# An attention, MoE and gated-MLP kernel: the first 768 tokens of its last layer by plain products in place of seven block products

## The chip, the cores and the metric

The kernel runs on one core of a Trainium2 chip. The metric is the device time of one execution in microseconds (us). The engines are TensorE (PE, its weight loads PEld), VectorE (DVE), ScalarE (ACT), GpSimd (POOL) and SyncE (SP), whose queue issues nearly all DMAs; each runs its own instructions in order.

## The reference

Windowed causal attention (4 x 8 heads, 576 tokens, head width 64) gives x, 2304 tokens x 512. Then come two feed-forward layers:

```python
# MoE1: 8 experts, each with the 288 tokens that the routing gives it
h = np.maximum(x[mask] @ w1[e], 0.0)      # 512 -> 1024
out[mask] = h @ w2[e]                     # 1024 -> 512
# MoE2: all 2304 tokens; its weights w_in, w_out arrive as 64-bit floats
h = x @ w_in                              # 512 -> 2048
g = h * (1.0 / (1.0 + np.exp(-h)))        # silu
return (g @ w_out).astype(np.float32)     # 2048 -> 512
```

## The kernel before

**Arithmetic.** Every float32 operand of a matmul is split into a high and a low part (`hi` by a ScalarE copy, `lo` by a VectorE subtraction), and a product takes three matmuls (`three`, L613 to L615; `unit`, L832).

**MoE1** (`moe1`) runs over 8 experts x 8 chunks of the hidden layer. A chunk (512 KB: a piece of w1 and one of w2) is loaded into a `raw` tile, split (`fetch`, L587 to L590, in a ring of 5 tiles), multiplied with the expert's 288 tokens (`first`, 12 matmuls, L762), put through relu (L765, L766), and two chunks later multiplied by its w2 piece (`second`, 12 matmuls of 288 columns). At each expert's end four accumulators are copied out (L783 on VectorE, L785 on ScalarE, two each) and stored to `yd` in DRAM.

**64-bit weights.** MoE2's 16 chunks are 64-bit. `fetch64` makes float32 of half a chunk: a 512 KB load (L600), then four VectorE operations (L604, L605, L606, L608) and one ScalarE Square (L607). Twelve chunks are converted during MoE1, one in every five steps, and kept in SBUF (`keep`, 12 tiles); four are converted during MoE2's group 0 (`late`) and go to `wd` in DRAM (L678), from where `chunk` reloads them (L667). The load, a `raw` tile, shares four `raw` slots with the chunks of MoE1, the block weights' temporary `s`, reloaded chunks and the output tiles.

**MoE2** (`moe2`) takes the tokens in three groups of 768. x @ w_in is made by seven block products instead of eight: `split_y` makes seven operands of a group's tokens (B11, B21, T1 to T4, B22; subtractions at L654, parts at L657 and L658), `split_w` seven of a pair of chunks (f and f + 8; sums on GpSimd L696 to L699, parts L692, L693). In group 0 `split_w` computes them and stores them to `wx` (L702, L703); groups 1 and 2 load them from there (L705, L706). A step (g, f) has seven products of 6 matmuls with 384 columns, in the order 0, 1, 3, 2, 4, 5, 6, in two PSUM tiles `pa` and `pb`; between them VectorE adds up the blocks (L890 to L907), so a product can't start before the sum over the product that last used its PSUM tile. Two silus of 768 columns follow (`silu`: sigmoid L848, product L849, copy L851, subtraction L852). Each step leaves 12 units (3 matmuls of 512 columns each, accumulating g @ w_out) in a list `todo`; `fill` runs them between the products of the next step:

```python
product(0, pa); ...; product(1, pb); fill(2)
product(3, pa); ...; fill(3)
product(2, pb); product(4, pa); ...; fill(4)
product(5, pa); product(6, pb); ...; fill(3)
```

Group 0's first step has no units pending; its products 0 and 1 are issued in MoE1, before the last `second`. A group's last units copy out the accumulators and scatter them to the output (L839 to L843).

**Order.** A planner places the instructions on each engine by its own estimate of times, in program order where it sees no better; instructions under `keep_in_program_order` stay in order among themselves. Each engine, and SP's queue, then runs that list strictly in order.

Of the kernel before, what the change touches and what calls it, by code (L numbers as in the profile page):

```python
# [20 lines left out]
P = 128  # L21
# [3 lines left out]
E = 8  # L25
# [596 lines left out]
HF = FC2 // 2  # L622
SOON = 6
BUSY_G = (14, 3, 3, 6)


class Halves:
# [19 lines left out]

    def split_y(self, n, sub=None):

        nc, b = self.tc.nc, self.b  # L650
        name = self.ORDER[n][1]
        for t, x, y, at in (("T1", "B12", "B11", "B11"), ("T2", "B22", "T1", "T1"), ("T3", "B22", "B12", "B12"), ("T4", "B21", "T2", "T2")):
            if name == t:
                (sub or nc.gpsimd).tensor_tensor(b[at], b[x], b[y], ALU.subtract)  # L654
                b[t] = b[at]
        hi, lo = (self.pool.tile([P, 2, HT], F32R, name=name + x) for x in "hl")
        nc.scalar.copy(hi, b[name])  # L657
        nc.vector.tensor_tensor(lo, b[name], hi, ALU.subtract)  # L658
        self.y[name] = hi, lo

    def chunk(self, c, n):

        q = slice(512 * n, 512 * n + 512)
        if c % HF < SOON:
            return self.f32[c][:, q]
        r = self.wts.raw.tile([P, 512], F32, name="raw")
        self.tc.nc.sync.dma_start(r, self.wd[c % HF - SOON + (HF - SOON) * (c // HF)][:, q])  # L667
        return r

    def convert(self, c):  # L670

        kept = c % HF < SOON
        r = self.f32[c] = self.wts.keep.tile([P, 1024], F32, name="w32") if kept else self.wts.raw.tile([P, 1024], F32, name="raw")
        self.wts.fetch64(c, r, (0,))
        yield
        self.wts.fetch64(c, r, (1,))
        if not kept:
            self.tc.nc.sync.dma_start(self.wd[c % HF - SOON + (HF - SOON) * (c // HF)], r)  # L678
# [39 lines left out]
def moe(tc, wts, xtab, idx96, k, hv, by128, idx128, out):  # L718
    nc = tc.nc
    with tc.tile_pool(name="ph", bufs=1, space=PSUM) as ph, tc.tile_pool(name="py", bufs=1, space=PSUM) as py, \  # L720
            tc.tile_pool(name="px", bufs=2, space=PSUM) as px:
        pp = [ph.tile([P, 512], F32, name=f"p{i}") for i in range(2)]
        w = moe1(tc, wts, xtab, idx96, k, hv, by128, pp, py, px)
        moe2(tc, wts, hv, w, idx128, out, pp, py, px)


def moe1(tc, wts, xtab, idx96, k, hv, by128, pp, py, px):
# [3 lines left out]
    with tc.tile_pool(name="m1", bufs=2) as m1:  # L731
# [39 lines left out]
        def second(e, f, h):  # L771
# [44 lines left out]
    return w0  # L816


def moe2(tc, wts, hv, w, idx128, out, pp, py, px):
    nc = tc.nc  # L820
    with tc.tile_pool(name="m2", bufs=1) as m2:
        obs = {}

        outs = dram_disjoint_views(out, NT)

        def unit(accs, g, f, blk, gg, z, d):

            (gh, gl), (hi, lo) = gg, z
            q = slice(d % 3 * P, d % 3 * P + P)
            start, stop = f == 0 and blk in (0, 1), f == HF - 1 and blk in (2, 3)  # L830
            for i, (x, y) in enumerate(((gh, hi), (gl, hi), (gh, lo))):
                tc.keep_in_program_order(nc.tensor.matmul(accs[d], x[:, q], y, start=start and i == 0, stop=stop and i == 2))  # L832
            if stop:
                if (g, d // 2) not in obs:
                    obs[g, d // 2] = wts.raw.tile([P, 2, 512], F32, name="raw")
                ob = obs[g, d // 2][:, d % 2]
                cut = 256 if f + 1 == HF and g + 1 == NG and d == 5 else 512 * (1 - d % 2)
                if cut:
# [6 lines left out]
        def silu(x):  # L845
# [20 lines left out]

        steps = [(g, f) for g in range(NG) for f in range(HF)]
        late = (x for i in range(2 * (HF - SOON)) for x in hv.convert(SOON + i // 2 + HF * (i % 2)))
        for i, (g, f) in enumerate(steps):
            if f == 0:  # L870
                accs = [py.tile([P, 512], F32, name=f"y{d}") if d < 4 else px.tile([P, 512], F32, name="pt") for d in range(6)]
            pa, pb = (p[:, 0:HT] for p in pp)

            def product(n, p):
                hv.product(n, p, w)
                if f == HF - 1 and g + 1 < NG:

                    for j in {2: (2, 3), 3: ()}.get(n, (n,)):
                        hv.split_y(j)

            if i:
                product(0, pa)
            u = hv.pool.tile([P, HT], F32, name="u")
            nc.scalar.copy(u, pa)
            if i:
                product(1, pb)
            fill(2)
# [22 lines left out]
            h21, h12 = silu(xb)  # L910
            order = [(0, h11, za, 0), (1, h22, zb, 3), (2, h21, zb, 0), (3, h12, za, 3)]
            if i + 1 < len(steps):
                w = hv.split_w(*steps[i + 1])
                todo += [(accs, g, f, b, h, z, d0 + d) for b, h, z, d0 in order for d in range(3)]
            else:

                for b, d in ((0, 0), (0, 1), (1, 3), (2, 0), (3, 3), (0, 2), (2, 1), (1, 4), (3, 4), (2, 2), (1, 5), (3, 5)):
                    _, h, z, d0 = order[b]
                    unit(accs, g, f, b, h, z, d)
            if g == 0:  # L920
                for _ in range((2, 1, 1, 2, 1, 1, 0, 0)[f]):
                    next(late)
            if f == 2 and g + 1 < NG:
                hv.load_y(g + 1)


@with_exitstack
def fused(ctx, tc, qT, kT, vA, vT, wg, w32, w64, rel, cst, out):
# [30 lines left out]
    c3.close()  # L959
    wts.keep = ctx.enter_context(tc.tile_pool(name="keep", bufs=2 * SOON))  # L960
# [3 lines left out]
    hv.wd = dram.tile([2 * (HF - SOON), P, 1024], F32, name="wd")  # L964

# [49 lines left out]
```

## Time and profile before

| | |
|---|---|
| median of 3 runs | 832.88 us (831.89 to 833.85) |
| profiled execution | 832.89 us |
| its span, first to last instruction | 831.1 us |
| mean granted TensorE clock | 0.969 of 2.4 GHz |
| MoE1 | 200.8 to 430.1 us of the span |
| MoE2, group 0 / 1 / 2 | from 430.1 / 560.2 / 688.2 us, last matmul near 824 us |

A stage here begins with its first matmul, and group 0's with the end of MoE1's last one. "Busy" TensorE includes overlapped matmuls, so the pace of a stage is read from the distance of its matmuls. "Idle before" is idle time of the engine ahead of an instruction, with what ended it.

### The profile page before, as it was taken

Reading aid. Unit: us, or ns where it says so; the run is one execution under the profiler, and the core shown is the slowest. Engines: PE = TensorE matmul, PEld = TensorE weight load, DVE = VectorE, ACT = ScalarE, POOL = GpSimd, SP = SyncE. Lnnn points to the kernel's source line nnn. Section 1 sums busy time; section 2 is a strip of 40 time slices with the busy share of each in tenths; the row PEclk is TensorE's granted clock in tenths of the full one; section 3 lists DMA queues with packets and bytes.
Section 4 is the critical chain, followed back from the end, with each engine's and each line's share of the span. In section 5 each row is a group of like instructions: output and inputs, shape, how many; then the busy total and the mean of one; then the engine's idle time right before and its main releaser. Section 6 shows DMA issues by size and latency. Waiting matters only on the chain.

```text
span 831.1 us, 13442 instructions
## 1 busy us (share of the span) xinstructions
PE 785.6 (95%) x4885; PEld 711.1 (86%) x4885; DVE 609.0 (73%) x1372; ACT 379.2 (46%) x659; POOL 219.8 (26%) x229
## 2 busy tenths in 40 slices
PE   7999999997999999999988999999999999999996
PEld 5899998746999999999977888888889888889885
DVE  7999899463677789887798897798555488556553
ACT  4967777202555554554544543454233245223222
POOL 3879799404011012000052111134000023100002
PEclk8999999597999999999998999999999999999999
DMA  9999773302686787778756355546534223723202
GB/s 233 292 249 239 204 216 110 123 2 71 196 271 221 234 305 237 238 268 295 249 183 251 140 205 172 193 173 215 207 100 167 89 88 131 262 90 137 92 0 77
DMA packets 48822, 150.14 MB, mean 181 GB/s; under 512 B 5808, under 2 KB 10416, under 8 KB 45680
## 3 DMA queue, kind: packets, MB, share of 16 engines
q1 hardware_dynamic: 45776, 139.79, 52.3%
q0 software_dynamic: 2976, 9.44, 3.3%
q8 instruction: 41, 0.67, 0.3%
q14 instruction: 29, 0.24, 0.1%
HBM read 118.28 MB, written 30.93 MB: 180 GB/s over the span
## 4 chain that ended last, share of the span: by engine, by line
PE 39%; DVE 17%; DMA 13%; issue 3%; ACT 3%; SPq 0%; POOLq 0%; POOL 0%; ACTq 0%; DVEq 0%
PE y L832 11%; DMA raw<-w 11%; PE pt L832 6%; PE p L613 5%; PE p L615 5%; PE p L614 5%; PE p L762 4%; DVE w L590 2%; DVE gl L852 2%; DVE w L693 2%; ACT w L589 2%; DVE bits L605 1%; DVE bits L606 1%; DVE sg L849 1%; PE y L614 1%
## 5 line engine op out<-in xcount | busy, mean ns | idle before, releaser
L832 PE MATMUL y<-z,gh 128*128 128x512 f32 x384 | 135.8, 395 | 0.0
L590 DVE TENSOR_TENSOR w<-raw,w 128x1024 fp32r<-128x1024 f32 x60 | 73.9, 1231 | 33.1 <-ACT w L589 32.6
L762 PE MATMUL p<-xh,w 128*128 128x288 f32 x512 | 82.3, 300 | 8.0 <-DVE hl L766 7.7
L589 ACT CAST w<-raw 128x1024 fp32r<-128x1024 f32 x60 | 63.0, 1049 | 55.7 <-DMA raw<-w 42.0
L832 PEld LDWEIGHTS y<-z,gh 128*128 128x128 f32 x384 | 72.6, 189 | 13.4 <-ACT gh L851 0.2
L762 PEld LDWEIGHTS p<-xh,w 128*128 128x128 f32 x512 | 72.0, 190 | 10.3 <-DVE hl L766 9.5
L832 PE MATMUL y<-z,gl 128*128 128x512 f32 x192 | 76.6, 399 | 3.5 <-DVE gl L852 3.5
L848 ACT ACTIVATE sg<-xa 128x768 f32<-128x768 f32 x24 | 20.3, 846 | 124.0 <-DVE xa L901 123.9
L614 PE MATMUL y<-hl,w 128*128 128x288 f32 x256 | 74.6, 298 | 0.6 <-DVE hl L766 0.6
L615 PE MATMUL y<-hh,w 128*128 128x288 f32 x256 | 73.9, 295 | 0.0
L832 PE MATMUL pt<-z,gh 128*128 128x512 f32 x192 | 71.2, 392 | 0.0
L613 PE MATMUL y<-hh,w 128*128 128x288 f32 x256 | 67.8, 300 | 1.5 <-ACT yo L785 1.1
L742 POOL DMA_INDIRECT xg<-xtab,idx x24 | 26.0, 1084 | 131.9 <-PE pt L746 123.0
L237 ACT ACTIVATE pe<-sc,mx 128x128 f32<-128x128 f32 x144 | 47.8, 395 | 20.7 <-DVE mx L235 20.4
L843 POOL DMA_INDIRECT out<-raw,idx x18 | 19.8, 1099 | 135.1 <-ACT raw L839 130.9
L852 DVE TENSOR_TENSOR gl<-sg,gh 128x768 fp32r<-128x768 f32 x48 | 52.4, 1092 | 2.2 <-ACT gh L851 2.2
L260 PE MATMUL po<-va,pc 128*128 128x73 f32 x256 | 53.0, 291 | 0.0
L260 PE MATMUL po<-va,pp 128*128 128x73 f32 x256 | 52.4, 289 | 0.3 <-DVE va L206 0.2
L614 PEld LDWEIGHTS y<-hl,w 128*128 128x128 f32 x256 | 48.5, 189 | 0.8 <-DVE hl L766 0.8
L654 POOL TENSOR_TENSOR yr<-yr 128x768 f32<-128x768 f32 x8 | 17.3, 2156 | 120.5 <-issue 92.6
L615 PEld LDWEIGHTS y<-hh,w 128*128 128x128 f32 x256 | 48.5, 189 | 0.0
L227 PE MATMUL pss<-khh,qs 128*128 128x256 f32 (+1 forms) x144 | 43.4, 322 | 4.0 <-DVE qs L141 3.6
(266 smaller groups left out, 2148.1 us busy)
## 6 DMA issues: line engine op xcount, KB each, us to landing
raw<-w SPq DMA_DIRECT2D x96, 512.0 KB, 4.8
w<-wx SPq DMA_DIRECT2D x16, 1024.0 KB, 4.9
w<-wx SPq DMA_DIRECT2D x16, 768.0 KB, 6.8
kr<-kT SPq DMA_DIRECT2D x35, 256.0 KB, 5.4
wx<-w SPq DMA_DIRECT2D x8, 1024.0 KB, 4.9
wx<-w SPq DMA_DIRECT2D x8, 768.0 KB, 5.1
va<-vA SPq DMA_DIRECT2D x18, 292.0 KB, 5.2
qr<-qT SPq DMA_DIRECT2D x18, 256.0 KB, 5.8
```

Of the source, the lines that this page charges most:

```text
L227: nc.tensor.matmul(pss[:, j, :nb, :], qs[:, h, :], kk[:, first:first + (nb - 1) * st + 1:st, h, :], start=(i == 0), stop=(i == 1))
L237: nc.scalar.activation(pe[:, i, :], sc[:, i, :], AF.Exp, bias=mx[:, i:i + 1], scale=-1.0)
L260: nc.tensor.matmul(po[:, j, :], w[:, j, :], va[:, s, 4 * g + j, :], start=(i == 0), stop=(i == nb - 1))
L589: nc.scalar.copy(hi, r)
L590: nc.vector.tensor_tensor(lo, r, hi, ALU.subtract)
L613: keep(tc.nc.tensor.matmul(out, whi, xhi, start=start, stop=False))
L614: keep(tc.nc.tensor.matmul(out, whi, xlo, start=False, stop=False))
L615: keep(tc.nc.tensor.matmul(out, wlo, xhi, start=False, stop=stop))
L742: nc.gpsimd.indirect_dma_start(xg, None, xtab, bass.IndirectOffsetOnAxis(ap=idx96[:, e * PER + j:e * PER + j + 1], axis=0))
L762: nc.tensor.matmul(p, w[:, dc * P:dc * P + P], x[:, dc, :], start=(i + dc == 0), stop=(i == 2 and dc == DC - 1))
L832: tc.keep_in_program_order(nc.tensor.matmul(accs[d], x[:, q], y, start=start and i == 0, stop=stop and i == 2))
L852: nc.vector.tensor_tensor(gl, sg, gh, ALU.subtract)
```

## The change

Group 0 of MoE2 no longer uses block products. It runs over the 16 chunks j; for each half t of the 768 tokens `plain` makes 12 matmuls of 384 columns, then come 3 units, and a silu of 384 columns (`silu1`), whose 3 units run after the next half's product. The chunk's split parts come from `fetch`, which now goes on past MoE1's 64 chunks. The seven operands of the tokens and `split_w`'s sums are made for group 1 first; group 0 needs four parts of its tokens without subtractions (`part_y`). Eight chunks (0 to 7) are converted in MoE1, one in seven steps, with load tiles of their own (two in the pool `m1`), and kept; the other eight are converted during group 0, 16 halves spread over j = 0 to 12, and all go to `wd`. `raw` has five slots. In MoE1 all four output copies are ScalarE's. Each output tile of MoE2 has a `raw` slot of its own instead of half of one. Operands B11 and B21 of a next group get a second buffer and are made two steps before its start.

```diff
     def fetch(self, upto):
-        while self.next < min(upto, E * FC1):
+        while self.next < min(upto, NW):
             i = self.next
-            r = self.raw.tile([P, 1024], F32, name="raw")
-            nc.sync.dma_start(r, self.w32[i])
+            if i < E * FC1:
+                r = self.raw.tile([P, 1024], F32, name="raw")
+                nc.sync.dma_start(r, self.w32[i])
+            else:
+                r = self.f32[i - E * FC1]
             hi, lo = self.parts(self.ring)
...
-    def fetch64(self, i, dst, halves=(0, 1)):
+    def fetch64(self, i, dst, raw, halves=(0, 1)):
...
-            r = self.raw.tile([P, 512, 2], I32, name="raw")
+            r = raw.tile([P, 512, 2], I32, name="raw")
...
-SOON = 6
+SOON = 8
...
+    def part_y(self, name, room=None):
+        nc = self.tc.nc
+        hi, lo = (self.pool.tile([P, 2, HT], F32R, name=(room or name) + x, bufs=2 if name in ("B11", "B21") else 1) for x in "hl")
+        nc.scalar.copy(hi, self.b[name])
+        nc.vector.tensor_tensor(lo, self.b[name], hi, ALU.subtract)
+        self.new[name] = hi, lo
...
     def chunk(self, c, n):
-        if c % HF < SOON:
-            return self.f32[c][:, q]
+        if c < SOON:
+            return self.wts.f32[c][:, q]
...
+    def plain(self, j, out, w, t):
+        hi, lo = w
+        for i in range(2):
+            yh, yl = self.y[f"B{i + 1}{t + 1}"]
+            for dc in range(2):
+                q = slice((2 * i + dc) * P, (2 * i + dc) * P + P)
+                three(self.tc, out, hi[:, q], lo[:, q], yh[:, dc], yl[:, dc], i + dc == 0, i + dc == 2, True)
...
     def split_w(self, g, f):
-        if g == 0:
+        if g == 1:
...
 def moe1(tc, wts, xtab, idx96, k, hv, by128, pp, py, px):
...
                 for d in range(DC):
-                    if d % 2:
-                        nc.vector.tensor_copy(yo[:, d], ys[e][d])
-                    else:
-                        nc.scalar.copy(yo[:, d], ys[e][d])
+                    nc.scalar.copy(yo[:, d], ys[e][d])
...
-                if n % 5 == 4 and n // 10 < SOON:
-                    for _ in hv.convert(n // 10 + HF * (n // 5 % 2)):
+                if n % 7 == 4 and n // 7 < SOON:
+                    for _ in hv.convert(n // 7, m1):
...
-                if n > 44 and n % 2 and n // 2 < 22 + 7:
-                    hv.split_y(n // 2 - 22, nc.vector)
-                if n == E * FC1 - 2:
-                    w0 = hv.split_w(0, 0)
+                if n in (46, 50, 54, 58):
+                    x = ("B11", "B21", "B12", "B22")[(n - 46) // 4]
+                    hv.part_y(x, "T4" if x == "B12" else None)
...
-        hv.product(0, pp[0][:, 0:HT], w0)
-        hv.product(1, pp[1][:, 0:HT], w0)
+        hv.plain(0, pp[0][:, 0:HT], wts.ready[E * FC1], 0)
...
 def moe2
...
-                if (g, d // 2) not in obs:
-                    obs[g, d // 2] = wts.raw.tile([P, 2, 512], F32, name="raw")
-                ob = obs[g, d // 2][:, d % 2]
+                ob = wts.raw.tile([P, 512], F32, name="raw")
...
+        late = (x for c in range(SOON, FC2) for x in hv.convert(c, wts.raw))
+        ahead = 0
+        for j in range(FC2):
+            while ahead < 2 * (FC2 - SOON) and ahead * 13 // 16 <= j:
+                next(late)
+                ahead += 1
+            wts.fetch(E * FC1 + j + 3)
+            hi, lo = wts.ready[E * FC1 + j]
+            z = hi[:, 512:], lo[:, 512:]
+            for t, p in enumerate((pa, pb)):
+                if j + t:
+                    hv.plain(j, p, (hi, lo), t)
+                fill(3)
+                h = silu1(p)
+                todo += [(accs, 0, h, z, 3 * t + d, j == 0, j == FC2 - 1) for d in range(3)]
+            if j == 3:
+                hv.load_y(1)
+            if j in (8, 9, 11, 12, 13):
+                hv.split_y((0, 1, 2, 3, 4)[(8, 9, 11, 12, 13).index(j)])
+            if j == 14:
+                w = hv.split_w(1, 0)
+        hv.split_y(5)
+        hv.split_y(6)
...
-        steps = [(g, f) for g in range(NG) for f in range(HF)]
+        steps = [(g, f) for g in range(1, NG) for f in range(HF)]
...
-            if g == 0:
-                for _ in range((2, 1, 1, 2, 1, 1, 0, 0)[f]):
-                    next(late)
             if f == 2 and g + 1 < NG:
                 hv.load_y(g + 1)
+            if f in (HF - 3, HF - 2) and g + 1 < NG:
+                hv.split_y(f - HF + 3)
...
-    wts.raw = ctx.enter_context(tc.tile_pool(name="raw", bufs=4))
+    wts.raw = ctx.enter_context(tc.tile_pool(name="raw", bufs=5))
```

## Rows read from the trace of the kernel before

**Rows 1.** The page's busy times: us, share of the span, instructions.

```profile
PE 785.6 (95%) x4885; PEld 711.1 (86%) x4885; DVE 609.0 (73%) x1372; ACT 379.2 (46%) x659; POOL 219.8 (26%) x229
```

**Rows 2.** Windows by stage: length, busy us (instructions) by engine, clock, DMA.

```profile
200.80:430.10 229.30, 219.25 (x1638) 215.43 (x1638) 180.36 (x274) 119.00 (x197) 30.30 (x28) 0.99 0.71 238
430.10:560.20 130.10, 121.40 (x580) 105.31 (x579) 110.04 (x159) 57.53 (x86) 28.59 (x27) 0.97 0.55 194
560.20:688.20 128.00, 125.95 (x626) 112.82 (x625) 82.41 (x116) 45.87 (x66) 15.63 (x10) 1.00 0.43 148
688.20:824.00 135.80, 134.34 (x661) 119.35 (x659) 78.44 (x115) 44.71 (x65) 13.12 (x11) 1.00 0.31 110
```

**Rows 3.** The chain that ended last, pieces: start us, us, what.

```profile
344.72 0.90 PE pt L746 x8
...
364.57 1.58 PE p L762 x12
...
571.00 2.06 PE y L832 x9
...
586.67 2.06 PE y L832 x9
```

**Rows 4.** Windows of 20 us, in the same columns as rows 2.

```profile
300.00:320.00 20.00, 16.85 (x125) 16.33 (x124) 17.97 (x27) 13.06 (x23) 5.28 (x4) 0.98 0.70 251
310.00:330.00 20.00, 18.36 (x129) 18.14 (x130) 18.73 (x29) 11.08 (x19) 5.60 (x4) 0.91 0.73 232
410.00:430.00 20.00, 16.68 (x116) 15.80 (x115) 16.23 (x21) 9.24 (x16) 8.99 (x9) 1.00 0.35 138
430.00:450.00 20.00, 15.17 (x63) 12.29 (x61) 18.16 (x30) 9.53 (x16) 4.82 (x6) 0.83 0.91 321
```

**Rows 5.** Timeline at group 0's first step: start us, us, instruction, idle before.

```profile
437.98 0.68 ACT L607 ACTIVATE raw<-raw 128x512 f32<-128x512 f32 x1 [5.02 <-DMA raw<-w]
...
438.56 0.83 ACT L848 ACTIVATE sg<-xa 128x768 f32<-128x768 f32 x1
```

**Rows 6.** VectorE's groups by line in MoE1: busy us, mean ns, idle before.

```profile
L590 DVE TENSOR_TENSOR w<-raw,w 128x1024 fp32r<-128x1024 f32 x59 | 72.7, 1232 | 33.1 <-ACT w L589 32.6
...
L605 DVE SCALAR_TENSOR_TENSOR bits<-raw,bits 128x512 int32<-128x512 int32 x24 | 17.2, 717 | 0.2
...
L604 DVE TENSOR_SCALAR bits<-raw 128x512 int32<-128x512 int32 x24 | 10.2, 427 | 0.0
L783 DVE COPY yo<-y 128x288 f32<-128x288 f32 x15 | 6.3, 451 | 0.0
L654 DVE TENSOR_TENSOR yr<-yr 128x768 f32<-128x768 f32 x4 | 3.8, 956 | 0.0
...
L658 DVE TENSOR_TENSOR B11l<-yr,B11h 128x768 fp32r<-128x768 f32 x1 | 1.0, 958 | 2.0 <-ACT B11h L657 2.0
```

**Rows 7.** TensorE's waits in MoE1: us in total, times, longest.

```profile
PE y L613 <- ACT yo L785: 1.1, 2, 0.7
```

**Rows 8.** ScalarE's groups by line in group 0's stretch.

```profile
L607 ACT ACTIVATE raw<-raw 128x512 f32<-128x512 f32 x8 | 5.4, 677 | 24.6 <-DMA raw<-w 24.6
L884 ACT COPY u<-p 128x384 f32<-128x384 f32 x7 | 3.3, 467 | 0.0
```

**Rows 9.** VectorE's groups by line in group 0's stretch.

```profile
L890 DVE TENSOR_TENSOR xa<-p,u 128x384 f32<-128x384 f32 x8 | 4.4, 551 | 0.0
```

**Rows 10.** SP queue's waits, whole span: us in total, times, longest.

```profile
SPq L678 <- DVE raw L608: 23.0, 4, 11.7
```

**Rows 11.** ScalarE's groups by line in MoE1.

```profile
L607 ACT ACTIVATE w<-raw 128x512 f32<-128x512 f32 x23 | 15.5, 675 | 29.7 <-DMA raw<-w 29.7
```

**Rows 12.** Timeline at the change from group 0 to group 1.

```profile
546.37 1.86 POOL L654 TENSOR_TENSOR yr<-yr 128x768 f32<-128x768 f32 x1 [12.27 <-DVE B11l L658]
...
546.67 2.37 DVE L852 TENSOR_TENSOR gl<-sg,gh 128x768 fp32r<-128x768 f32 x1
```

More of the change, by code (lines that the diff above doesn't have):

```diff
@@ L561, in __init__ @@
         self.raws = []
+        self.f32 = {}
     def parts(self, pool):
@@ L653, in split_y, with convert @@
             if name == t:
-                (sub or nc.gpsimd).tensor_tensor(b[at], b[x], b[y], ALU.subtract)
+                nc.gpsimd.tensor_tensor(b[at], b[x], b[y], ALU.subtract)
                 b[t] = b[at]
[L656 to L659, printed above, removed]
+        self.part_y(name)
     def chunk(self, c, n):
         q = slice(512 * n, 512 * n + 512)
-        if c % HF < SOON:
-            return self.f32[c][:, q]
+        if c < SOON:
+            return self.wts.f32[c][:, q]
         r = self.wts.raw.tile([P, 512], F32, name="raw")
-        self.tc.nc.sync.dma_start(r, self.wd[c % HF - SOON + (HF - SOON) * (c // HF)][:, q])
+        self.tc.nc.sync.dma_start(r, self.wd[c - SOON][:, q])
         return r
[L670 to L674, printed above, removed]
+    def convert(self, c, raw):
+        r = self.wts.f32[c] = self.wts.keep.tile([P, 1024], F32, name="w32") if c < SOON else raw.tile([P, 1024], F32, name="raw")
+        self.wts.fetch64(c, r, raw, (0,))
         yield
-        self.wts.fetch64(c, r, (1,))
-        if not kept:
-            self.tc.nc.sync.dma_start(self.wd[c % HF - SOON + (HF - SOON) * (c // HF)], r)
+        self.wts.fetch64(c, r, raw, (1,))
+        if c >= SOON:
+            self.tc.nc.sync.dma_start(self.wd[c - SOON], r)
         yield
+    def plain(self, j, out, w, t):
[5 more added lines that the diff above has]
+                three(self.tc, out, hi[:, q], lo[:, q], yh[:, dc], yl[:, dc], i + dc == 0, i + dc == 2, True)
     def split_w(self, g, f):
@@ L722, in moe @@
         pp = [ph.tile([P, 512], F32, name=f"p{i}") for i in range(2)]
-        w = moe1(tc, wts, xtab, idx96, k, hv, by128, pp, py, px)
-        moe2(tc, wts, hv, w, idx128, out, pp, py, px)
+        moe1(tc, wts, xtab, idx96, k, hv, by128, pp, py, px)
+        moe2(tc, wts, hv, idx128, out, pp, py, px)
 def moe1(tc, wts, xtab, idx96, k, hv, by128, pp, py, px):
@@ L807, in moe1, with moe2, unit @@
                     hv.load_y(0)
-                if n > 44 and n % 2 and n // 2 < 22 + 7:
-                    hv.split_y(n // 2 - 22, nc.vector)
-                if n == E * FC1 - 2:
-                    w0 = hv.split_w(0, 0)
+                if n in (46, 50, 54, 58):
+                    x = ("B11", "B21", "B12", "B22")[(n - 46) // 4]
+                    hv.part_y(x, "T4" if x == "B12" else None)
+        hv.y, hv.new = hv.new, {}
         second(*pend.pop(0))
-        hv.product(0, pp[0][:, 0:HT], w0)
-        hv.product(1, pp[1][:, 0:HT], w0)
+        hv.plain(0, pp[0][:, 0:HT], wts.ready[E * FC1], 0)
         second(*pend.pop(0))
-    return w0
-def moe2(tc, wts, hv, w, idx128, out, pp, py, px):
+def moe2(tc, wts, hv, idx128, out, pp, py, px):
     nc = tc.nc
     with tc.tile_pool(name="m2", bufs=1) as m2:
-        obs = {}
         outs = dram_disjoint_views(out, NT)
-        def unit(accs, g, f, blk, gg, z, d):
+        def unit(accs, g, gg, z, d, start, stop):
             (gh, gl), (hi, lo) = gg, z
             q = slice(d % 3 * P, d % 3 * P + P)
-            start, stop = f == 0 and blk in (0, 1), f == HF - 1 and blk in (2, 3)
             for i, (x, y) in enumerate(((gh, hi), (gl, hi), (gh, lo))):
@@ L833, in unit @@
             if stop:
-                if (g, d // 2) not in obs:
-                    obs[g, d // 2] = wts.raw.tile([P, 2, 512], F32, name="raw")
-                ob = obs[g, d // 2][:, d % 2]
-                cut = 256 if f + 1 == HF and g + 1 == NG and d == 5 else 512 * (1 - d % 2)
+                ob = wts.raw.tile([P, 512], F32, name="raw")
+                cut = 256 if g + 1 == NG and d == 5 else 512 * (1 - d % 2)
                 if cut:
@@ L853, in silu, with silu1 @@
             return [(gh[:, i], gl[:, i]) for i in range(2)]
+        def silu1(p):
+            sg = m2.tile([P, HT], F32, name="sg", bufs=1)
+            nc.scalar.activation(sg, p, AF.Sigmoid)
+            nc.vector.tensor_tensor(sg, p, sg, ALU.mult)
+            gh, gl = (m2.tile([P, HT], F32R, name=n, bufs=3) for n in ("gh", "gl"))
+            nc.scalar.copy(gh, sg)
+            nc.vector.tensor_tensor(gl, sg, gh, ALU.subtract)
+            return gh, gl
         def split2(src):
@@ L876, in product @@
                 if f == HF - 1 and g + 1 < NG:
-                    for j in {2: (2, 3), 3: ()}.get(n, (n,)):
+                    for j in {2: (2, 3), 4: (4,), 5: (5,), 6: (6,)}.get(n, ()):
                         hv.split_y(j)
-            if i:
-                product(0, pa)
+            product(0, pa)
             u = hv.pool.tile([P, HT], F32, name="u")
             nc.scalar.copy(u, pa)
-            if i:
-                product(1, pb)
+            product(1, pb)
             fill(2)
@@ L910, in moe2 @@
             h21, h12 = silu(xb)
-            order = [(0, h11, za, 0), (1, h22, zb, 3), (2, h21, zb, 0), (3, h12, za, 3)]
+            order = [(h11, za, 0, f == 0, False), (h22, zb, 3, f == 0, False), (h21, zb, 0, False, f == HF - 1),
+                     (h12, za, 3, False, f == HF - 1)]
             if i + 1 < len(steps):
                 w = hv.split_w(*steps[i + 1])
-                todo += [(accs, g, f, b, h, z, d0 + d) for b, h, z, d0 in order for d in range(3)]
+                todo += [(accs, g, h, z, d0 + d, start, stop) for h, z, d0, start, stop in order for d in range(3)]
             else:
                 for b, d in ((0, 0), (0, 1), (1, 3), (2, 0), (3, 3), (0, 2), (2, 1), (1, 4), (3, 4), (2, 2), (1, 5), (3, 5)):
-                    _, h, z, d0 = order[b]
-                    unit(accs, g, f, b, h, z, d)
-            if g == 0:
-                for _ in range((2, 1, 1, 2, 1, 1, 0, 0)[f]):
-                    next(late)
+                    h, z, d0, start, stop = order[b]
+                    unit(accs, g, h, z, d, start, stop)
             if f == 2 and g + 1 < NG:
                 hv.load_y(g + 1)
+            if f in (HF - 3, HF - 2) and g + 1 < NG:
+                hv.split_y(f - HF + 3)
+            if f == HF - 1:
+                hv.y = dict(hv.new)
 @with_exitstack
@@ L959, in fused @@
     c3.close()
-    wts.keep = ctx.enter_context(tc.tile_pool(name="keep", bufs=2 * SOON))
+    wts.keep = ctx.enter_context(tc.tile_pool(name="keep", bufs=SOON))
     wts.late = ctx.enter_context(tc.tile_pool(name="late", bufs=1))
```

15 lines of the change are left out of this document (9 added, 6 removed).

## The prediction

> **What bounds the kernel now.** I read the page's busy times first. TensorE is busy for 785.6 of 831.1 us, VectorE for 73% [rows 1]. The reader is to see only that TensorE is the engine to follow; where it loses time, a whole-span share doesn't tell. So the span was cut into stages (MoE1, then MoE2's groups 0, 1, 2) [rows 2], and each stage compared with the pace that the chain of waits shows where nothing disturbs it [rows 3].
>
> The pace: a block-product step takes 586.67 - 571.00 = 15.67 us. Nine 512-column matmuls take 2.06, so 0.229 each and 8.2 for a step's 36; its 42 matmuls of 384 columns share the other 7.4, 0.177 each. Twelve 288-column ones take 1.58, 0.132 each; eight transposes 0.90.
>
> MoE1 at that pace: 1536 x 0.132 = 202.8, seven gathers of 12 transposes 9.5, two products of group 0 that run in it 2.1: 214.4. It lasts 229.3, so 14.9 are lost. A group is 8 x 15.67 = 125.4. Group 0's stretch holds that less the 2.1 and less the twelve units (8.2) that run at the start of group 1: 115.1 of 130.1 us, 15.0 lost. Group 1 loses 128.0 - 125.4 = 2.6, group 2 135.8 - 133.6 = 2.2. In all 34.7 us, 30 of them in the two stages in which 64-bit chunks are converted and VectorE is 79% and 85% busy; in group 1 it is at 64%.
>
> Three places hold half of it [rows 4]. At 300 to 320 us TensorE idles 3.2 us, and after it the clock is granted at 0.91 over 20 us (2.4 GHz, and 1.2 for some of it: 1.8 us); there VectorE makes group 0's seven operands, subtractions included. At 410 to 430 it idles 3.3: conversions and the first block weights. At 430 to 450, group 0's first step, it idles 4.8 and the clock is at 0.83 (3.4 us): no units are pending there, so every sum of blocks lies open. The timeline of ScalarE shows why that step is so slow: it stands 5.0 us at a Square (L607) whose chunk has not landed, and the sigmoid queued behind it starts right after it [rows 5].
>
> **The change, part by part.**
>
> *The plain product.* Group 0 makes 16 x 24 = 384 matmuls of 384 columns in place of 8 x 42 = 336. 48 x 0.177 = +8.5 us on TensorE, with nothing to hide it. The units stay 288.
>
> *MoE1.* Eight half chunks leave. A half is 0.427 + 3 x 0.717 = 2.58 us of VectorE [rows 6], so 20.6. Seven parts and four subtractions (0.958 and 0.956) become four parts: -6.7. Sixteen output copies of 0.451 go to ScalarE: -7.2. Block weights give way to three whole chunk splits: about -2. VectorE falls from 180 to 144 us, some two thirds of the stage. So I count the 3.2 + 1.8 + 3.3 = 8.3 us of the first two places as returned. Both bounds: none of it, if other waits set the end; all 14.9 at most. Against it, ScalarE copies all four outputs at each expert's end; TensorE waited for such copies for 1.1 us in two places [rows 7], so I add 0.5 (0 to 4.9, seven ends at 0.7). Chunk loads get a fifth slot, and conversions two of their own: 1 us (0 to 3). Left: 14.9 - 8.3 + 0.5 - 1 = 6.1.
>
> *Group 0, start.* The first plain product is issued before MoE1's last second layer (1.6 us), and the product for the other half (2.1 us) covers the rest of its silu. Of the 8.2 us lost there now I leave 0.5; above, 8.2.
>
> *Group 0, each j.* A half-j is 12 x 0.177 + 9 x 0.229 = 4.2 us, and a silu must be done in 4.2. Its four steps on 384 columns: sigmoid 0.47 and copy 0.47, by ScalarE's 384-column copy; product with PSUM 0.55, by L890 [rows 8, 9]; subtraction 0.48, half of a part's. That is 2.0, and leaves 2.2 us for handovers and whatever stands ahead in the queues of ScalarE and VectorE. VectorE per j: split 1.23, silu 2.1, conversions 16/13 x 2.58 = 3.2: 6.5 of 8.4 us. So silu fits unless an instruction ahead of it waits. The one that does is the moved conversion. There are now 16 halves here, not 8: 16 loads of 512 KB and 8 writes to wd on SP's queue, past which nothing goes. A write waits for its second half, and SP stood at four of them for 23.0 us [rows 10], with the next load behind it. ScalarE then stands at the Square, sigmoid behind it, TensorE's next units behind that. Today that wait is 29.7 / 23 = 1.3 us in MoE1 and 24.6 / 8 = 3.1 us in group 0 [rows 8, 11]. The first is within the 2.2, the second 0.9 beyond it, plus some 0.4 if the handovers take a fifth of the room. Bounds per half: 0 and 1.3. Group 0 loses its 14 MB of wx writes (8 x 1.75 MB) and gets 8.4 MB of conversions for 4.2, so it moves less than now; MoE1 is the nearer row. I take 0.22, 3.5 us in all.
>
> *Group 0, operands of group 1.* Four subtractions on GpSimd and seven parts fall into j = 8 to 15. A VectorE subtraction that takes 0.96 took 2.37 while GpSimd ran such a one [rows 12]: four times 1.4, mostly beside TensorE's work; 0.5 on the path, 0 to 5.6. [...]
>
> *Group 1.* The block weights are made here, and the open step moves here: three units are pending at its start, where twelve were. Its sums lie open once, before the sixth product (0.55 plus handover, 0.8). The first units then need two sums (1.1) and a silu of 768 columns (0.83 + 1.1 + 0.83 + 0.96, twice the pieces above): 4.8, against 0.8 and four products (4.2) on TensorE. That is level, so queues and handovers show; I take 1.2. In all 2.0 us, against 8.2 in the old place, since no conversion stands ahead (upper bound 8.2). The seven other steps lost (15.0 - 8.2) / 7 = 1.0 in group 0 with conversions; without them I take 0.5: 3.5. VectorE gets 110 - 8 x 2.6 = 89 of some 131 us. Eight chunks, not four, come back from wd, 256 KB at a time, ahead by a step. B11 and B21 are made two steps early, which shortens the end: 0.5. Sum 6.0, from 3 to 14. *Group 2* keeps 1.5 of 2.2.
>
> Sum: losses 6.1 + 4.5 + 6.0 + 1.5 = 18.1 in place of 34.7, so 16.6 back, 8.5 paid: -8.1. The profiled execution took 832.89 (span 831.1), and the median of the runs is 832.88, so both give **824.8 us**.
>
> **Rivals.**
>
> *Conversions stop group 0* (the other side). Place: the Square ahead of the sigmoid. If all 16 halves wait 3.1 us as today, they cost 16 x 1.3 = 20.8, not 3.5: 842. It decides from 3.5 + 8.1 = 11.6 us, 0.73 a half, a mean wait of some 2.5 us. For it: today's 3.1, and twice the writes on SP's queue. Against: that queue also waited for wx writes that leave. As a case 833 to 842.
>
> *MoE1 is not VectorE's.* ScalarE's casts and Squares wait for loads, and losses merely move: MoE1 keeps 13, time 831.7. For it: 29.7 us of Square waits in MoE1 [rows 11]; against: the stalls lie where VectorE is full [rows 4].
>
> *Everything is covered*: losses of 9 in all, as the 2 to 3 us of groups 1 and 2 today would give: 832.9 + 8.5 - 25.7 = 815.7. Against it: the open step and the 16 conversions.
>
> *TensorE is the bound and the change only loads it*: nothing comes back, 832.9 + 8.5 = 841.4. For it TensorE's 95%; against it the 34.7 us in which it does not keep its own pace. The Trainium skill (Perfetto Trace Analysis, Identifying the Most-Contended Engine) says to judge TensorE by weight loads, not by matmul occupancy, and to relieve the most-contended engine first; by that rule this change adds to it. The stage rows speak for gaps instead, so it gets little.
>
> **How the numbers follow.** Chances: forecast 0.42 (820 to 830), all covered 0.18, MoE1 unchanged 0.15, conversions 0.19, bound alone 0.06. One can tell this kernel from no change at about 0.2%, 1.7 us. Faster: 0.41 + 0.18 + 0.06 = 0.65. Within it: 0.01 + 0.08 + 0.03 = 0.12. Slower: 0.16 + 0.01 + 0.06 = 0.23. The range 813 to 840 leaves out about 0.04 below and 0.12 above.
>
> **What would show it.** Right: 384 plain matmuls at 0.177 us; MoE1 shorter by 7 to 11 us, with no stall at group 0's operands; the half-j at 4.2 us with gaps of a few tenths; the open step at group 1's start, 2 to 3 us; Squares of group 0 waiting under 2 us. Wrong: Square waits near 3 us with TensorE idle for gl or gh after them; MoE1 stalls of the same sum at other places; group 1 steps near 17 us, or a granted clock below 1 after its first step.

## The result, and the profile after

The kernel after takes 839.92 us (median of 20 runs, 834.03 to 850.77), the kernel before 832.96 (20 runs, 828.95 to 840.67): a ratio of 1.0075, 95% interval 1.0053 to 1.0097. The change makes the kernel slower by 0.75%. The prediction said 824.8 us and faster; its range, up to 840, holds the time by a hair and by luck, and its direction is wrong. The profiled execution took 836.94 us, span 835.2.

The busy line of the page, in the form of [rows 1], still says little: TensorE 94%, VectorE a little lower than before.

```profile
PE 788.1 (94%) x4933; PEld 719.2 (86%) x4933; DVE 586.6 (70%) x1325; ACT 394.5 (47%) x696; POOL 220.9 (26%) x229
```

There are 48 more matmuls, as forecast. The windows by stage answer to [rows 2]; below them are three stretches within the stages, in the same columns as [rows 4].

```profile
198.40:418.20 219.80, 215.81 (x1638) 215.05 (x1638) 160.39 (x223) 123.59 (x202) 28.53 (x24) 0.99 0.66 217
418.20:556.00 137.80, 133.04 (x655) 118.85 (x653) 91.92 (x146) 58.64 (x102) 3.91 (x4) 0.99 0.33 108
556.00:688.50 132.50, 123.33 (x599) 109.87 (x598) 97.12 (x131) 54.81 (x82) 42.56 (x37) 0.97 0.49 177
688.50:828.10 139.60, 136.03 (x661) 120.63 (x659) 78.37 (x114) 44.79 (x65) 13.85 (x11) 0.99 0.32 113
...
300.00:320.00 20.00, 19.66 (x150) 19.67 (x151) 17.13 (x26) 12.28 (x23) 2.82 (x3) 1.00 0.77 243
...
560.00:570.00 10.00, 5.30 (x26) 4.83 (x24) 5.08 (x6) 1.85 (x3) 5.04 (x5) 0.88 0.86 314
570.00:580.00 10.00, 7.17 (x26) 5.73 (x24) 8.79 (x11) 5.22 (x9) 9.84 (x9) 0.78 0.33 112
```

TensorE's own pace, from the same prices as in the prediction, is 214.4 us for MoE1. A j of group 0 is 24 x 0.177 + 18 x 0.229 = 8.37, so group 0 is 16 x 8.37 - 4.2 = 129.7 (a product and three units fall outside its stretch). Group 1 starts with three units pending and leaves twelve, 125.4 + 2.1 - 8.2 = 119.3, and group 2 is 133.6. Together that is 597.0. The stages last 629.7. So they lose 5.4, 8.1, 13.2 and 6.0 us, 32.7 in all, where the prediction had 6.1, 4.5, 6.0 and 1.5, in all 18.1. Of the 34.7 us lost before, 2.0 came back and 8.5 were paid. That makes the stages 6.5 us longer, and the span 4.1, since MoE1 begins 2.4 us earlier in this execution. MoE1 did what was forecast; the losses of groups 1 and 2 are new.

The timeline shows where (the bracket is the idle time before an instruction and what ended it; the text counts most stalls of TensorE from the starts of its matmuls, 0.1 to 0.3 us more):

```profile
379.99 4.74 POOL L666 TENSOR_TENSOR yr<-yr 128x768 f32<-128x768 f32 x2 [42.71 <-DVE B11l L657]
380.69 2.33 DVE L609 SCALAR_TENSOR_TENSOR bits<-raw,bits 128x512 int32<-128x512 int32 x1
...
383.32 2.49 DVE L594 TENSOR_TENSOR w<-raw,w 128x1024 fp32r<-128x1024 f32 x1
...
387.72 2.74 POOL L666 TENSOR_TENSOR yr<-yr 128x768 f32<-128x768 f32 x1 [2.99 <-DVE T1l L657]
...
388.70 2.30 DVE L612 SCALAR_TENSOR_TENSOR w<-w,bits 128x512 f32<-128x512 f32 x1
...
390.49 0.83 ACT L656 CAST T2h<-yr 128x768 fp32r<-128x768 f32 x1 [3.06 <-POOL yr L666]
...
392.30 0.93 PE L779 MATMUL p<-xh,w 128*128 128x288 f32 x5 [2.78 <-DVE hl L783]
...
417.34 1.62 ACT L799 COPY yo<-y 128x288 f32<-128x288 f32 x4 [1.45 <-PE y L619]
418.88 0.49 ACT L867 ACTIVATE sg<-p 128x384 f32<-128x384 f32 x1
...
423.02 0.50 PE L843 MATMUL y<-w,gl 128*128 128x512 f32 x1 [1.23 <-DVE gl L871]
...
466.13 1.22 DVE L594 TENSOR_TENSOR w<-raw,w 128x1024 fp32r<-128x1024 f32 x1
467.27 0.55 DVE L871 TENSOR_TENSOR gl<-sg,gh 128x384 fp32r<-128x384 f32 x1
...
564.73 0.69 DVE L850 COPY raw<-pt 128x512 f32<-128x512 f32 x1 [1.67 <-DMA out<-raw,idx]
...
565.86 0.83 ACT L656 CAST B11h<-yr 128x768 fp32r<-128x768 f32 x1 [5.58 <-DMA yr<-yd]
...
566.73 0.96 DVE L657 TENSOR_TENSOR B11l<-yr,B11h 128x768 fp32r<-128x768 f32 x1 [1.31 <-ACT B11h L656]
567.60 0.55 DVE L947 TENSOR_TENSOR xb<-p,xa 128x384 f32<-128x384 f32 x1
...
568.21 0.69 PE L617 MATMUL p<-T4h,w 128*128 128x384 f32 x1 [4.70 <-DVE xb L947]
...
708.93 0.59 ACT L848 COPY raw<-pt 128x512 f32<-128x512 f32 x1 [5.26 <-DMA out<-raw,idx]
709.42 0.85 ACT L857 ACTIVATE sg<-xb 128x768 f32<-128x768 f32 x1
...
711.20 0.69 PE L617 MATMUL p<-T2h,w 128*128 128x384 f32 x1 [2.15 <-ACT u L932]
```

Read it by place.

**380 us, the end of MoE1.** GpSimd makes the subtractions of group 1's operands here. The program writes these operands from j = 8 of group 0 on and the subtractions from j = 11, over 100 us later; the planner has moved them up. (L608 to L612 are the steps of a 64-bit conversion.) Beside the first two, a step on VectorE takes 2.33 us, not 0.69, with MoE1's relu behind it, and TensorE stalls for 0.9 us; a split takes 2.49, not 1.22. The third takes 2.74 us, with another step stretched to 2.30. ScalarE stands 3.1 us for its result, with relu's first half behind that cast, and TensorE stalls for 2.9.

**417 and 466 us, group 0.** ScalarE makes four output copies before the first sigmoid, and the first units stall for 0.8 and 1.5. Later `gl` stands behind a split on VectorE (466.13) and stalls the units for 1.3; at 520 us it stands behind a conversion step, both stretched beside GpSimd's sums of block weights, and stalls them for 1.7.

**563 to 568 us, group 1's first step.** TensorE stands 4.7 us for a sum (L947). Two instructions wait ahead of that sum on VectorE: a copy of group 0's sixth output tile, which has no `raw` slot until an earlier tile's scatter has landed, and then B11l. That B11 is group *2's*: its tokens' load was moved up, too, and lands at 565.8. After the stall the granted clock is 0.88 and 0.78 in place of 1.00.

**709 us, group 2's second step.** ScalarE stands 5.3 us at an output copy for such a slot, with the sigmoid and `u` behind it. SP's queue waits for such slots, too (its waits, whole span: us in total, times, longest):

```profile
SPq L676 <- DMA out<-raw,idx: 23.6, 8, 9.2
```

ScalarE's waits at the Squares, the prediction's main fear, are small; this row answers to [rows 8], whose eight halves waited 24.6 us:

```profile
L611 ACT ACTIVATE raw<-raw 128x512 f32<-128x512 f32 x16 | 10.8, 678 | 15.3 <-DMA raw<-w 15.3
```

That is 0.96 us a half, under the 2.2 that the prediction allowed.

### The profile page after: what moved, and what is told of

It is laid out like the page before. It is cut to its first block, busy times and chain, and to the rows that moved or that the text cites. A ratio compares the mean times of both kernels' runs of the same rounds, so it can differ in the third digit from the quotient of the medians.

```text
span 835.2 us, 13505 instructions
## 1 busy us (share of the span) xinstructions
PE 788.1 (94%) x4933; PEld 719.2 (86%) x4933; DVE 586.6 (70%) x1325; ACT 394.5 (47%) x696; POOL 220.9 (26%) x229
## 4 chain that ended last, share of the span: by engine, by line
PE 49%; DVE 11%; DMA 9%; issue 3%; ACT 2%; POOL 1%; SPq 0%; POOLq 0%; DVEq 0%; ACTq 0%
PE y L843 10%; PE p L779 10%; PE pt L843 5%; PE p L617 5%; PE p L619 5%; PE p L618 4%; DMA raw<-w 4%; PE y L618 3%; PE y L619 3%; PE y L617 3%; DMA yr<-yd 3%; DMA yd<-yo 2%; DVE bits L609 1%; DVE bits L610 1%; DVE raw L612 1%
## 5 line engine op out<-in xcount | busy, mean ns | idle before, releaser
L594 DVE TENSOR_TENSOR w<-raw,w 128x1024 fp32r<-128x1024 f32 x68 | 84.9, 1249 | 40.0 <-ACT w L593 38.2
L593 ACT CAST w<-raw 128x1024 fp32r<-128x1024 f32 x68 | 71.5, 1051 | 48.8 <-PE y L619 46.5
L843 PE MATMUL y<-z,gh 128*128 128x512 f32 x256 | 90.2, 394 | 0.0
L619 PE MATMUL y<-hh,w 128*128 128x288 f32 x256 | 74.9, 297 | 0.0
L617 PE MATMUL y<-hh,w 128*128 128x288 f32 x256 | 70.7, 301 | 0.0
L857 ACT ACTIVATE sg<-xa 128x768 f32<-128x768 f32 x16 | 13.6, 847 | 95.8 <-DVE xa L948 95.8
L843 PEld LDWEIGHTS y<-z,gh 128*128 128x128 f32 x256 | 48.5, 189 | 9.1 <-ACT gh L860 0.2
L843 PE MATMUL y<-z,gl 128*128 128x512 f32 x128 | 51.0, 398 | 3.4 <-DVE gl L861 3.4
L713 POOL TENSOR_TENSOR raw<-raw 128x256 f32<-128x256 f32 x8 | 7.1, 886 | 160.3 <-DVE bits L610 120.1
L619 PEld LDWEIGHTS y<-hh,w 128*128 128x128 f32 x256 | 48.6, 190 | 0.0
L843 PE MATMUL pt<-z,gh 128*128 128x512 f32 x128 | 47.4, 392 | 0.0
L617 PEld LDWEIGHTS y<-hh,w 128*128 128x128 f32 x256 | 46.8, 192 | 0.0
```

The costliest lines, as they stand in the source:

```text
L617: keep(tc.nc.tensor.matmul(out, whi, xhi, start=start, stop=False))
L619: keep(tc.nc.tensor.matmul(out, wlo, xhi, start=False, stop=stop))
```

## The experiments

The theory was that three things which the prediction had not costed carry the loss: operands made too early, a `raw` slot for each output tile, and four copies on ScalarE at MoE1's end. The rival was the prediction's own, the conversions in group 0. All ratios are to the kernel before on the same chip, with their 95% intervals.

**e1: output tiles in pairs**, as before the change.

```diff
-                ob = wts.raw.tile([P, 512], F32, name="raw")
+                if (g, d // 2) not in obs:
+                    obs[g, d // 2] = wts.raw.tile([P, 2, 512], F32, name="raw")
+                ob = obs[g, d // 2][:, d % 2]
```

> The changed kernel with one edit: two output tiles share a raw slot again, three slots a group instead of six. Theory A (the output tiles fill the five raw slots, each for the 7 us of its scatter, and a ScalarE or VectorE copy that waits for a slot stops the silu and sums behind it): the 5.3 us wait of the output copy at 709 us and the 1.7 us wait at 565 us go, with the late chunk loads behind them, so group 2 loses some 4 us less and group 1's first two steps 2 to 4 less: 832 to 834 us, near the kernel before. Theory B (the operands of the next group, made too early, are what stops it): at most 1 us, 838 to 840. The planner orders the rest anew, so each reading is to be taken at its place in the trace.

836.37 us, ratio 1.0044 (1.0017 to 1.0070), about 2.6 us better than after. That is not clear of noise (the two ratios differ by 0.0031, give or take 0.0035) and short of what its theory asked. In the trace, group 2's stall is gone. Group 1's first step still stands as long for its sum: with the slot there, VectorE waits for B11h alone.

```profile
577.35 0.69 PE L617 MATMUL p<-T4h,w 128*128 128x384 f32 x1 [4.53 <-DVE xb L950]
```

**e2: the loads of groups 1 and 2 held** in program order.

```diff
-        self.tc.nc.sync.dma_start(r, self.yd....)
+        ld = self.tc.nc.sync.dma_start(r, self.yd....)
+        if g:
+            self.tc.keep_in_program_order(ld)
```

> The changed kernel with one edit: the token loads of groups 1 and 2 keep their place in SP's program order, so that operands can't be made before them. In the changed kernel group 1's five operands and three GpSimd subtractions were made in MoE1 (378 to 396 us) and group 2's first ones in group 1's first step. Theory B (these early operands stop VectorE and ScalarE): the MoE1 stalls of 0.9 and 2.9 us and the clock of 0.83 behind them go (5.5 us), and of the 4.9 us stall in group 1's first step some 3: 831 to 834 us. Theory A (output tiles): the MoE1 part alone, 835 or more, and the 5.3 us ScalarE wait at the start of group 2 stays.

837.19 us, ratio 1.0071 (1.0041 to 1.0102): nothing gained, against its theory, though MoE1 loses the stalls at its end (it lasts 215.4 us). The operands now follow the load at once, into group 0, where the same stretching hits the silu (timeline):

```profile
448.39 4.57 POOL L668 TENSOR_TENSOR yr<-yr 128x768 f32<-128x768 f32 x2 [109.54 <-DVE B11l L659]
...
449.09 2.17 DVE L873 TENSOR_TENSOR gl<-sg,gh 128x384 fp32r<-128x384 f32 x1
451.18 2.06 DVE L608 TENSOR_SCALAR bits<-raw 128x512 int32<-128x512 int32 x1
```

Holding the load alone is not enough.

**e3: MoE1's output copies shared** by VectorE and ScalarE, as before.

```diff
-                    nc.scalar.copy(yo[:, d], ys[e][d])
+                    if d % 2:
+                        nc.vector.tensor_copy(yo[:, d], ys[e][d])
+                    else:
+                        nc.scalar.copy(yo[:, d], ys[e][d])
```

> The changed kernel with one edit: VectorE again makes two of MoE1's four output copies of each expert. Theory C (four copies in a row on ScalarE stand ahead of group 0's first sigmoid, 417.3 to 418.9 us): the stall of 2.3 us at group 0's start shrinks by 1 and the clock drop of 1.7 us behind it may go: 1 to 2.7 us, 837 to 839 us. If the copies don't matter: 840 within 1 us. VectorE gets 7 us more in MoE1, with no effect there expected.

834.41 us, ratio 1.0045 (1.0017 to 1.0074), about 2.5 us better, as asked, but again not clear of noise. Its group 0 stalls for 1.7 us at the start in place of 2.3, and after that keeps 8.4 us in nearly every j, with all 16 conversions in it: against the rival.

**e4: the three together.**

> All three edits: output tiles in pairs, token loads held, copies shared. If theories A, B and C name the whole difference between the forecast and the result: the forecast's 825 us, to 829; group 1's first step still lies open with three units pending, so 2 to 4 us of stall stay there. If the early operands and slots are only where the wait shows and the open step costs as much without them: 833 to 836.

831.12 us, ratio 0.9992 (0.9961 to 1.0022). Back to the time before and not to the forecast's 825: operands still crowd group 0 at 453 to 459 us, and group 1's third step.

**e5: e1 and e3, and the parts held**, with the loads free.

```diff
-        nc.scalar.copy(hi, self.b[name])
+        self.tc.keep_in_program_order(nc.scalar.copy(hi, self.b[name]))
...
-                nc.gpsimd.tensor_tensor(b[at], b[x], b[y], ALU.subtract)
+                self.tc.keep_in_program_order(nc.gpsimd.tensor_tensor(b[at], b[x], b[y], ALU.subtract))
```

> The changed kernel with output tiles in pairs, copies shared, and the operands' parts and GpSimd subtractions (not the loads) held in program order: group 1's at j = 8 to 13 of group 0, group 2's in steps 5, 6 and 7 of group 1. Theory D (what costs is a part that waits for its token load ahead of silu and sums; placed well behind the load it costs nothing): no wait of ScalarE for yr, no stall above 1 us at the parts, 826 to 828 us. Theory E (what costs is a GpSimd subtraction that shuts VectorE out for its 2 us, wherever it stands): stalls of 2 to 5 us move to j = 11 to 15, 830 to 833 us, as with the loads held.

822.87 us, ratio 0.9931 (0.9903 to 0.9958): the first that beats the kernel before, and faster than either theory said.

**e6: e5 with these subtractions on VectorE** (`nc.gpsimd` becomes `nc.vector` in that line).

> The same, with the eight subtractions for groups 1 and 2 on VectorE, 0.96 us each, in place of GpSimd's 2.2. Theory E: VectorE's instructions of 2.0 to 2.6 us at the operands go, and the stalls beside them: 2 to 5 us less than with GpSimd, 826 to 828. Theory D or neither: the same time within 1.5 us, since VectorE gets 7.6 us of work and loses some 10 us of stretch.

818.85 us, ratio 0.9861 (0.9826 to 0.9897). That is 4.0 us less than e5, as theory E asked, so it was not only the place of the operands. A subtraction takes 0.95 us there (1.5 once), and 1.8 to 2.3 on GpSimd in e5.

**e7: e6 with group 0's units two halves later**, **e8: the kernel after with that edit alone.** Three units are left over when the next half's three are added.

```diff
-                fill(3)
+                fill(max(0, len(todo) - 3))
```

> The same as the run with the subtractions on VectorE, and group 0's units run two halves later, not one: a silu then has 8.4 us in place of 4.2, and six units are pending at the start of group 1, not three. If silu's room in group 0 and the open step hold what is left: group 0's steps all at 8.4 us (2 to 4 us less) and 1 to 2 us less in group 1's first step: 823 to 825. If they don't: the same within 1.5 us.

> The changed kernel with the later units as its only edit. If silu's room is what failed in the forecast (conversions ahead of the sigmoid, my second side): the stalls of 1.3 and 1.7 us at 466 and 518 us and that of 2.3 at group 0's start go with their clock drop, 5 to 8 us: 832 to 835. If output tiles and early operands are: at most 3 us, 837 to 839.

e7: 816.17 us, ratio 0.9847 (0.9811 to 0.9882), no clear gain over e6. e8: 831.57, ratio 1.0022 (0.9999 to 1.0045), about 4.4 better than after. In both, group 0 has no stall over 0.3 us. But e7 has a new one, the only large one left (timeline, then a window of 10 us):

```profile
545.01 0.37 SPq L650 DMA_DIRECT2D yr<-yd  x1
545.49 11.62 SPq L676 DMA_DIRECT2D raw<-wd  x4
...
562.21 0.69 PE L617 MATMUL p<-T2h,w 128*128 128x384 f32 x1 [6.18 <-ACT w L709]
```

```profile
560.00:570.00 10.00, 7.43 (x22) 6.06 (x23) 6.41 (x7) 4.58 (x7) 5.38 (x7) 0.55 0.85 297
```

Group 2's tokens, 1.5 MB, are loaded ahead of four chunk loads of 256 KB, one of them for the block weights of group 1's second step. These are late, and the clock falls to a mean of 0.55, so 1.2 GHz for nine tenths of these 10 us.

**e9: the kernel after with e5's held parts alone.**

> The kernel after, with one edit: the ScalarE copy that opens an operand and the GpSimd subtraction of two blocks keep their place in the program, as they do in the kernel with five edits; nothing else is undone. Theory (operands made too early are the largest of the uncosted terms): the 2.9 us stall at the end of MoE1 and the 4.9 us in group 1's first step go, 831 to 835 us and a ratio to the kernel before of 0.997 to 1.003. Rival (the output tiles' slots and the crowd of copies at MoE1's end carry it, and the operands only fill a wait that is there anyway): 837 us or more, with stalls of the same sum in the same two places.

827.83 us, ratio 0.9974 (0.9946 to 1.0003): 0.0101 of ratio, or 8.4 us, better than after from this edit alone, more than the theory asked for. The edit holds group 0's four parts as well (at 353 to 392 us; 295 to 300 in after, beside a stall of 0.5), so a little of the gain may be theirs. By stage (windows, columns of [rows 2]):

```profile
200.50:414.10 213.60, 213.60 (x1638) 213.52 (x1638) 149.92 (x218) 119.99 (x197) 18.49 (x20) 1.00 0.68 224
414.10:551.20 137.10, 132.22 (x654) 117.37 (x653) 97.03 (x150) 60.73 (x105) 10.20 (x8) 1.00 0.32 108
551.20:678.50 127.30, 121.56 (x598) 107.39 (x597) 96.19 (x129) 54.89 (x82) 45.63 (x38) 1.00 0.51 182
678.50:817.10 138.60, 134.79 (x661) 119.09 (x659) 80.00 (x117) 45.54 (x67) 12.88 (x11) 1.00 0.33 114
```

MoE1 is at its pace, TensorE busy in all of it, and group 1 is 5.2 us shorter than in after.

**e10: e7 with group 2's load held** (e2's edit, for `g == 2` only).

> The last kernel (output tiles in pairs, shared copies, held parts, subtractions on VectorE, units two halves later), with the load of group 2's 512 tokens of 1.5 MB kept in its place in the program. Theory (the 6.3 us stall ahead of group 1's second step comes from four chunk loads that stand behind that load on SP's queue): the stall falls under 2 us, TensorE's clock stays above 0.9 in 560 to 570 us, and the time is 806 to 812 us, ratio 0.972 to 0.980. Rival (the chunks are late because their raw slots come free late, whatever is ahead of them in the queue): the stall stays at 4 to 6 us, the time at 815 to 818.

811.11 us, ratio 0.9763 (0.9727 to 0.9799), the best version. The stall is 0.4 and 0.9 us and the clock stays (windows):

```profile
199.10:412.90 213.80, 213.80 (x1640) 213.68 (x1639) 155.46 (x233) 115.93 (x182) 18.20 (x20) 1.00 0.68 223
412.90:540.70 127.80, 127.80 (x645) 116.01 (x645) 96.50 (x154) 59.87 (x103) 4.24 (x4) 1.00 0.36 120
540.70:666.20 125.50, 122.93 (x607) 109.06 (x606) 97.22 (x133) 54.73 (x82) 37.53 (x34) 1.00 0.50 181
666.20:801.20 135.00, 134.11 (x661) 119.38 (x660) 78.93 (x118) 46.19 (x67) 11.62 (x10) 1.00 0.32 117
...
560.00:570.00 10.00, 9.89 (x49) 8.75 (x50) 9.03 (x14) 4.80 (x8) 4.92 (x6) 1.00 0.93 348
```

The stages last 602.1 us; TensorE's pace is 597.0.

**e11: the kernel before, with all its subtractions on VectorE.** Is the gain the plain product's, or that of taking GpSimd off the operands?

```diff
-                (sub or nc.gpsimd).tensor_tensor(b[at], b[x], b[y], ALU.subtract)
+                nc.vector.tensor_tensor(b[at], b[x], b[y], ALU.subtract)
```

> The kernel before, with seven block products in all three groups, and one edit: the block subtractions of groups 1 and 2 are made by VectorE, not by GpSimd. Theory (the plain product is what the best kernel gains from): groups 1 and 2 lost only 2.6 and 2.2 us before, so at most 3 us come back, 829 to 833 us, ratio 0.996 to 1.000. Rival (the gain of the later kernels comes from taking GpSimd off the operands, and the plain product has no part in it): 823 us or less, ratio under 0.99.

825.10 us, ratio 0.9931 (0.9906 to 0.9956): between the two. By stage (windows):

```profile
197.20:427.70 230.50, 219.58 (x1639) 215.29 (x1638) 180.39 (x274) 118.77 (x197) 32.70 (x29) 0.99 0.72 237
427.70:555.80 128.10, 120.25 (x580) 104.57 (x579) 107.53 (x162) 57.29 (x86) 23.63 (x24) 0.99 0.56 198
555.80:681.60 125.80, 125.65 (x625) 112.82 (x624) 80.10 (x119) 45.80 (x67) 7.01 (x6) 1.00 0.42 150
681.60:816.30 134.70, 134.03 (x660) 119.37 (x659) 77.74 (x116) 45.05 (x66) 10.29 (x10) 1.00 0.30 110
```

GpSimd cost the kernel before some 5.7 us: groups 0, 1 and 2 are 2.0, 2.2 and 1.1 us shorter than there. But e10 is 14.0 us faster still, with MoE1 16.7 us shorter than here (213.8 against 230.5). That difference is the whole change with the other edits of e10; the plain product alone was not tried.

**e12: e10 with MoE1 converting four of its chunks a second time** into the same place.

```diff
+                if n in (8, 22, 36, 50):
+                    wts.fetch64(n // 7 - 1, wts.f32[n // 7 - 1], m1)
                 h = first(e, f)
```

> The last kernel (six edits), in which MoE1 converts four of its eight 64-bit chunks a second time into the same place, so that it makes as many half chunks as the kernel before: 8 more loads of 512 KB, 8 more Squares and 20.6 us more of VectorE in MoE1, with nothing else changed. Theory (MoE1 was held up by VectorE's conversions, as the prediction had it): MoE1 lasts 6 us or more longer than in the last kernel, and the time is 817 to 823 us, ratio 0.984 to 0.991. Rival (the stalls of the kernel before came from the seven operands and the block weights that MoE1 also made, and the conversions were hidden): MoE1 lasts no more than 2 us longer, the time stays at 811 to 814 us, ratio 0.976 to 0.980.

813.34 us, ratio 0.9795 (0.9762 to 0.9829), not clearly apart from e10. In the profiled execution MoE1 takes 3.7 us longer (window):

```profile
198.10:415.60 217.50, 215.26 (x1638) 213.82 (x1638) 171.45 (x265) 116.92 (x190) 21.91 (x20) 1.00 0.73 239
```

Between the theory's 6 and the rival's 2: eight half chunks, 8 x (0.42 + 3 x 0.69) = 20 us of VectorE, cost MoE1 about a quarter of the 14.9 us that it lost before. The rest must lie in what else changed there: subtractions, three parts and block weights left it, GpSimd's work with them, and `raw` got a fifth slot and the conversions load tiles of their own. Which of these held most was not tried.

## Why the prediction was wrong

*Plain product, +8.5:* right. 48 more matmuls; where nothing disturbs it a j takes 8.4 us, and the prices from [rows 3] give 8.37.

*MoE1, losses of 6.1:* right in size (5.4; the stage is 9.5 us shorter, where 7 to 11 were asked). The mechanism is right in part: 300 to 320 us is now busy for 19.7 of 20 at full clock, where it idled 3.2 us [rows 4], but of the conversions' share only 3.7 us is shown (e12). And the 5.4 that stay are not the leftovers of before: most are group 1's operands. With these gone the stage lasts 215.4 us (e2), and with group 0's parts held, too, it loses nothing (e9, e10). VectorE, counted at 144 us, is busy for 160.4 with these operands in it and for 149.9 without (e9).

*Operands of group 1, 0.5 on the path:* **the step that failed.** It put them where the program writes them, in j = 8 to 15 of group 0. They ran at 380 us, in MoE1, and those of group 2 at the start of group 1. Held in their place they give back 8.4 us (e9). The rows before held the warning: group 0's operands, written from the 46th of MoE1's 64 steps on (near 362 us, at 3.6 us a step), stand at 300 to 320 us [rows 4], over 40 us ahead of that place. So the planner already made operands as soon as it could. Group 1's T1 waited before until 546 us [rows 12], though its tokens' load was issued at 383, and the code names a reason: each operand had one buffer, and group 0's products read it until then. Group 0 now reads only four parts, and B11 and B21 have two buffers each. That the buffers held them is read from code and trace; no run gave the kernel before more buffers.

*Output tiles:* not costed at all, though the change's own description names the slot of each. An output tile's scatter lands some 7 us after its issue (median 7.2 in the kernel before, 7.1 at this place in e7), six tiles and the chunks share five slots, and SP's queue, too, stood 23.6 us for such slots. The stall that they cause goes with e1; its worth, 2.6 us, is not clear of noise. The prediction had even booked the fifth slot as a gain.

*Group 0, start, 0.5; MoE1's expert ends, 0.5:* too small. The prediction had the second half's product cover the first silu. Four output copies stood ahead of the sigmoid, a split and a conversion ahead of `gl`. Sharing the copies gives 2.5 (e3, not clear of noise); letting the units run two halves later, which also ends the stalls at 466 and 520 us, gives 4.4 (e8).

*Conversions in group 0, 3.5; the rival with 0.19:* the measured time lies near this rival's 842, but for other reasons. Squares waited 0.96 us a half, and e3 and e8 keep the pace with all 16 conversions in group 0. What cost time there was a conversion step or a split ahead of `gl` on VectorE, not a Square ahead of the sigmoid on ScalarE.

*Group 1, 6.0, and group 2, 1.5:* 13.2 and 6.0. The open step came where it was expected, but what closed it late was the copy and B11l ahead of its sum, more than its own sums: it takes 17.0 us, 12.9 with the operands held (e9) and 9.5 at TensorE's pace. So 5.2 of group 1's 13.2 are the operands', and the 8.0 left compare with the 6.0. The sign named in the prediction, steps near 17 us and a clock below 1, was seen (17.0 and 20.9 us). Group 2's loss falls to 1.4 in e10, which has the tiles in pairs and the parts held, about the 1.5 of the forecast.

The three separate gains, 8.4 (e9) + 4.4 (e8) + 2.6 (e1) = 15.4, are as large as the error, 839.9 - 824.8 = 15.1. That they match so well is luck: they need not add up (e1, e2 and e3 together gave 0.0083 of ratio, singly 0.0065), each is uncertain by some 3 us, and only those of e9 and e8 are clear of noise. What stays open is the share of the fall in clock: it came after each large stall, and no run separates it.

*The other rivals.* MoE1 did give back 9.5 us, so the rival by which it keeps a loss of 13 falls. "The bound is only loaded", 841.4, has the right time and the wrong reason: TensorE's pace is 597.0 us, and e10 comes within 5.1 of it. "Everything is covered", 815.7, is what the change reaches only with the edits: e7 and e10 take 816.2 and 811.1, with the later units and with VectorE's subtractions, which give the kernel before 5.7 us as well (e11).

## What to carry to other kernels

A change that frees buffers can let a planner move work forward, so ask of every producer what held it in its place until now; where the trace before shows work running far ahead of its line, it may happen again. Hold the compute that makes an operand, not only its load, and look at what stands behind each moved load on the DMA queue. Count the slots that outputs hold until they have landed, and price a moved step by what is next in the strict order of its engine.

## What the hardware showed unexpectedly

Beside a GpSimd subtraction, VectorE's conversion step with two inputs in SBUF went from 0.69 to 2.33 us, and the one with a single input (L608) from 0.42 to 2.06 (e2), while relu's `hl`, which reads PSUM, kept its 0.45 (at 382.95 us of after). The Trainium skill (SBUF — State Buffer, Who interferes with whom) makes it a lock for a whole instruction, taken by two SBUF inputs or by the two-port modes that a `tensor_scalar` can enter; these rows agree, though none shows in which mode L608 ran. So a silu whose product reads PSUM is not safe: its last subtraction, with two inputs in SBUF, took 2.17 us in place of 0.55 (at 449.09 of e2).
